# Gated linear attention with an ELU layer in float32: the output layer's matmuls regrouped, and a new written order for the first units

## The chip, the core and the metric

The kernel runs on one core of a Trainium2 chip. Its engines are TensorE (PE: matmul, with its weight loads listed apart as PEld), VectorE (DVE), ScalarE (ACT), GpSimd (POOL) and SyncE (SP), which here only issues DMAs. Each engine works through its own queue in order and waits on semaphores. The metric is the device time of one execution in microseconds (us); the figure to be forecast is the median over the runs.

## The reference

Shapes are B=4 sequences, H=8 heads, S=768 steps, D=48 channels; all in float32, with the two weight matrices given in float64.

```python
mag = np.sqrt(a_re * a_re + a_im * a_im)
scale = np.minimum(mag, 0.999) / (mag + 1e-06)
a_re_n, a_im_n = a_re * scale, a_im * scale
for t in range(S):                                   # complex decay per channel d
    new_re = ar * S_re - ai * S_im
    new_im = ar * S_im + ai * S_re
    S_re, S_im = new_re + k[t] (outer) v[t], new_im
    y[:, :, t] = q[t] @ S_re
x = y.transpose(0, 2, 1, 3).reshape(3072, 384)
h = x @ w_in                                         # 384 -> 2048
g = np.where(h > 0.0, h, np.exp(np.minimum(h, 0.0)) - 1.0)
out = g @ w_out                                      # 2048 -> 384
```

## The kernel before, in words

**Units.** The work is cut into 12 units (`NU`). A unit is 128 steps of two of the four sequences, so 256 tokens; `where(u)` says which. Units u and u+2 hold the same two sequences, one block of steps further on, so a unit needs the angles carried from unit u-2 (`carry`, a one-row DMA) and the states (`state`).

**One unit.** `squares` to `slopes`, `angles` and `carried` turn a_re, a_im into logarithms of magnitudes and angles. `decays` sums the logarithms over the steps with a triangular matmul (L873 for u>1, in `quartered`) and takes their exponentials E and F on ScalarE (L883). `turns` sums the angles the same way (L832) and DVE takes away whole turns; the result is `z`. `waves` makes sines and cosines on ScalarE (L949 to L953), `scaled` multiplies k by F and q by E, `gated` multiplies both by sine and cosine (kg, qg). `transposed` turns kg and qg over through TensorE (L984), with copies by ScalarE (L985). `scores` (L992), `states` (L1016, with updates on DVE at L1027 and POOL at L1029) and `values` (L1039, L1046) make the attention output for each sequence n; `seam` moves the last channels into place by DMA. `noted` records the least a_re and the largest |a_im| with two DVE reductions (unit 1: on ScalarE).

**The two layers.** `inner(u, f)` computes 256 hidden channels for the unit's 256 tokens: 6 matmuls of 256 columns (L1091) into one of three PSUM buffers named mlp. `elu(u, f)` takes two ScalarE steps and one on DVE (L1100 to L1102) into the tile g, of which a unit has two halves (`x["g", 0]`, `x["g", 1]`), from four buffers (tags g0 and g1, two each). `project(u, n, f0, f1)` is the output layer for the 128 tokens of sequence n: for each of 16 blocks f, one matmul with 128 weights columns of g and 384 columns of w_out (L1112), summed in one mlp buffer; then one ScalarE copy (L1118) and one store (L1120).

**Weights.** `fetch` loads float64 weights; `rounded` (called by `convert`, one DVE operation at a time, five for each of 16 chunks, L39 to L49 and L651) rounds them to float32. Later `test_fetch` loads all the weights a second time and `test` reduces them on DVE (L677): 16 pieces of 768 elements a partition, with two buffers. `verdict` combines what was noted; in the rare case that some value lies outside what the fast path takes, a general path behind an `If` runs instead. It doesn't run here.

**The order.** Nothing schedules the instructions but a list. `first` is written out by hand for units 0 to 2 and part of 3. All that follows comes from `plan`: every step has a place in slots (16 to a unit), and steps are issued in the order of their places: `decays_of`, `gates_of`, `values_of`, `layer_of`. Each engine's queue has its instructions in this order. `warm(n)` are matmuls without a use, to keep TensorE busy in the start.

Of the kernel before, what the change touches and what calls it, by code (L numbers as in the profile page):

```python
# [31 lines left out]
WF = 2  # L32

# [471 lines left out]
def kernel(  # L505
# [55 lines left out]
    NR = 2 * NI * NF // (NI * WF)  # L561
    seen = cst.tile([C, 2 * NU + NR], FP32, name="seen")
    least, smallest, most = seen[:, 0:NU], seen[:, NU : NU + NR], seen[:, NU + NR :]
    off = cst.tile([C, 2], FP32, name="off")
# [92 lines left out]
    def test_fetch(m):  # L657

        t = sb.tile([C, WF * DM, 2], U32, tag="w64", bufs=2, name="w64")
        if m < NR // 2:  # L660
            n = WF * DM // NI
            nc.sync.dma_start(
                out=t.rearrange("p (i n) two -> p i (n two)", i=NI),
                in_=moe_w_in[:, ds(2 * m * n, 2 * n)].rearrange("(i p) n -> p i n", p=C),
            )
        else:
            nc.sync.dma_start(
                out=t.rearrange("p (f n) two -> p f (n two)", f=WF),
                in_=moe_w_out[ts(m - NR // 2, WF * C)].rearrange("(f p) n -> p f n", p=C),
            )  # L670
        tested.append((m, t))
# [21 lines left out]
    def begun(u):  # L693
        keys = ("w", "m2", "sq", "t", "th", "z"), ("m2", "e", "sq", "w", "t", "th")
        for key in keys[u] if u < 2 else ("m2", "sq"):
            nat[u][key] = new("n", 6)

# [5 lines left out]
    def joined(u):  # L703

        x = nat[u]
        if u > 0:
            products(u).tensor_tensor(out=x["m2"], in0=x["m2"], in1=x["sq"], op=ALU.add)  # L707
            return
        x["both"] = [work([C, HD]) for n in range(NB)]
        for key in ("m2", "sq"):  # L710
            for n in range(NB):
                nc.tensor.matmul(
                    x["both"][n], lhsT=ident, rhs=flat(x[key][:, n : n + 1]),
                    start=(key == "m2"), stop=(key == "sq"),
                )

    def logarithms(u):
# [4 lines left out]
        if u == 0:  # L722
            for n in range(NB):
                nc.scalar.activation(
                    out=flat(lm[:, n : n + 1]), in_=x["both"][n], func=AF.Ln
                )
            return
# [5 lines left out]
    def powers(u):  # L733
        x = nat[u]
        if u == 0:
            x["e"] = x["m2"]
            for n in range(NB):
                nc.scalar.activation(
                    out=x["e"][:, n], in_=x["m2"][:, n], func=AF.Exp, scale=-0.5, bias=ln_eps
                )  # L740
# [8 lines left out]
    def ratios(u):  # L749
        x = nat[u]  # L750
        if u == 0:
            for n in range(NB):
                t = x["t"][:, n]
                nc.vector.tensor_tensor(out=t, in0=x["ai"][:, n], in1=t, op=ALU.mult)
            return
        w, t = x["w"], x["t"]
# [3 lines left out]
    def lengths(u):  # L760

        x = nat[u]
        if u == 0:
            nc.vector.tensor_scalar(
                out=x["w"], in0=x["m2"], scalar1=2 * float(np.log(CAP)), scalar2=None,
                op0=ALU.min,
# [15 lines left out]
    def noted(u, part=None):  # L782
# [3 lines left out]
        if u == 1:  # L786
            sq = nat[u]["sq"]
            for n, (x, scale, bias) in enumerate(((sq, 1.0, most_sq), (ar, -1.0, least_re))):
                nc.scalar.activation(
                    out=sq, in_=x, func=AF.Relu, scale=scale, bias=bias,  # L790
                    accum_out=off[:, n : n + 1],
                )
            return
        if part in (None, 0):
            nc.vector.tensor_reduce(
                out=least[:, u : u + 1], in_=flat(ar), axis=mybir.AxisListType.X, op=ALU.min
            )
        if part in (None, 1):
            nc.vector.tensor_reduce(
                out=most[:, u : u + 1], in_=flat(ai), axis=mybir.AxisListType.X, op=ALU.max,  # L800
                apply_absolute_value=True,
            )
# [3 lines left out]
    def angles(u):  # L806
        x = nat[u]
        if u == 0:
            for n in range(NB):
                nc.scalar.activation(out=x["th"][:, n], in_=x["t"][:, n], func=AF.Arctan)  # L810
# [15 lines left out]
    def turns(u):  # L826
        x = nat[u]
        if u > 0:
            x["z"] = new("n", 6)
        for n in range(NB):  # L830
            t = work([C, HD])
            nc.tensor.matmul(  # L832
                t, lhsT=sum_turns, rhs=x["th"][:, n].rearrange("p h d -> p (h d)"),
                start=True, stop=True,
            )
            r = new("rnd", 1, [C, HD])
            nc.vector.tensor_scalar(
                out=r, in0=t, scalar1=MAGIC, scalar2=MAGIC, op0=ALU.add, op1=ALU.subtract
            )
            nc.vector.tensor_tensor(  # L840
                out=x["z"][:, n].rearrange("p h d -> p (h d)"), in0=t, in1=r, op=ALU.subtract
            )
            if u < 2:
                if n == 0:
                    x["cs"] = new("cs", 1, [C, NB * H, 2, D])
                nc.vector.tensor_scalar(
                    out=x["cs"][:, n * H : (n + 1) * H, 0].bitcast(U32),
                    in0=x["z"][:, n].bitcast(U32), scalar1=0x7FFFFFFF, scalar2=None,
                    op0=ALU.bitwise_and,
                )  # L850
        nxt = u + B // NB
        if nxt < NU:
            carry[nxt] = new("carry", 2, [1, NB * HD])
            nc.gpsimd.dma_start(out=carry[nxt], in_=flat(x["z"])[C - 1 : C])  # L854

    def sums():
        x = nat[0]
        x["sums"] = [
            work([C, HD], "mlp") for n in range(NB)
        ]  # L860
        for n in range(NB):
            nc.tensor.matmul(
                x["sums"][n], lhsT=sum_logs, rhs=flat(x["w"][:, n : n + 1]),
                start=True, stop=False,
            )
# [26 lines left out]

    def decays(u):
# [443 lines left out]
```

## Time and profile before

| | |
|---|---|
| median of 9 runs | 726.92 us (723.76 to 732.7) |
| the profiled execution | 724.98 us, span 723.3 us |
| PE busy | 693.9 us (96%), 6240 records |
| PE weight loads busy | 512.0 us (71%) |
| DVE busy | 311.2 us (43%) |
| ACT busy | 398.5 us (55%) |
| POOL busy | 197.5 us (27%) |
| output layer (L1112) on PE | 768 records, 260.7 us busy |
| hidden layer (L1091) on PE | 1152 records, 262.6 us busy |

A float32 matmul stands in the trace as two records. A record's mean duration (491 ns for the output layer) holds its time in the pipeline; what it costs in a row of its like is the distance from one to the next, which the chain of work that ended last gives: a group's time by its count. "PE mlp L1112 x8" in the chain is eight records, four matmuls. In the groups of instructions, the columns are line, engine, operation, output<-inputs, shapes, count, then busy us and mean ns, and the idle time just before with what ended it. In the instructions in order of time: start us, us, engine, line, operation, output<-inputs, count, and in brackets the idle time before and what ended it.

### The profile page before, as it was taken

The numbers are of one execution on the slowest core, as the hardware profiler recorded it, in microseconds if no ns is written. First come the engines' busy times: TensorE is split into PE (matmuls) and PEld (weight loads), VectorE is DVE, ScalarE is ACT, GpSimd is POOL, SyncE is SP. The second block draws the span as 40 slices with busy tenths as digits, with TensorE's granted clock in tenths as the row PEclk, the third lists the DMA queues.
The fourth block names the chain that finished last, engine by engine and source line by source line (L and its number), as shares of the span: only waits on it lengthen the run. The fifth ranks groups of instructions, "written<-read, shape, count | busy, mean of one in ns | idle before, by whom it ended". The sixth has DMA issues, their size and how long they took to land.

```text
span 723.3 us, 14664 instructions
## 1 busy us (share of the span) xinstructions
PE 693.9 (96%) x6240; PEld 512.0 (71%) x6240; DVE 311.2 (43%) x426; ACT 398.5 (55%) x617; POOL 197.5 (27%) x207
## 2 busy tenths in 40 slices
PE   6889999977999999999999999999999999999996
PEld 4667785556866876876875875875885886786773
DVE  6889899554415324324324324423423323420120
ACT  6675361597466465565664674665666556550220
POOL 2000000056234134224324414414416306302000
PEclk9999999999999999999999999999999999999999
DMA  9964964430902902902902902812832722000000
GB/s 163 169 113 90 190 187 131 93 62 9 146 11 73 152 2 64 162 2 61 159 8 61 136 32 62 115 52 61 93 73 61 109 58 62 12 1 18 11 1 27
DMA packets 143110, 55.92 MB, mean 77 GB/s; under 512 B 128532, under 2 KB 132796, under 8 KB 143036
## 3 DMA queue, kind: packets, MB, share of 16 engines
q1 hardware_dynamic: 139456, 53.52, 39.2%
q0 software_dynamic: 3360, 1.22, 1.5%
q8 instruction: 51, 0.84, 0.5%
q14 instruction: 23, 0.19, 0.1%
q10 hardware_dynamic: 220, 0.14, 0.1%
HBM read 48.88 MB, written 4.78 MB: 74 GB/s over the span
## 4 chain that ended last, share of the span: by engine, by line
PE 84%; DVE 4%; SPq 3%; DMA 3%; issue 2%; POOL 2%; ACT 1%; ACTq 0%; POOLq 0%; DVEq 0%
PE mlp L1112 35%; PE mlp L1091 33%; PE w L984 5%; PE w L992 3%; PE w L1016 3%; PE y L1046 3%; SPq L594 2%; PE y L1039 2%; PE w L832 2%; DMA x<-y 1%; PE w L873 1%; DMA w<-in_moe_w_in_dram 1%; DMA w<-in_a_im_dram 1%; SPq L640 0%; POOL n L707 0%
## 5 line engine op out<-in xcount | busy, mean ns | idle before, releaser
L1091 PE MATMUL mlp<-x,w_in 128*128 128x256 f32 x1152 | 262.6, 383 | 3.2 <-DMA x<-y 1.9
L1112 PE MATMUL mlp<-w_out,g 128*128 128x384 f32 x768 | 260.7, 491 | 0.0
L1091 PEld LDWEIGHTS mlp<-x,w_in 128*128 128x128 f32 x1152 | 215.7, 191 | 35.4 <-issue 3.3
L1112 PEld LDWEIGHTS mlp<-w_out,g 128*128 128x128 f32 x768 | 142.1, 190 | 96.3 <-issue 4.8
L1102 DVE SCALAR_TENSOR_TENSOR g<-ee,mlp 128x512 f32<-128x512 f32 x96 | 65.9, 687 | 175.9 <-ACT ee L1101 162.9
L1100 ACT ACTIVATE ee<-mlp 128x512 f32<-128x512 f32 x96 | 57.4, 597 | 127.8 <-PE mlp L1091 123.3
L1029 POOL TENSOR_TENSOR S<-S,T 128x384 f32<-128x384 f32 x36 | 35.7, 992 | 183.3 <-DVE S L1027 183.3
L1101 ACT ACTIVATE ee<-ee 128x512 f32<-128x512 f32 x96 | 60.5, 630 | 2.9
L854 POOL DMA_DIRECT2D carry<-n x10 | 5.1, 506 | 159.2 <-DVE n L840 159.2
L1071 POOL DMA_DIRECT2D x<-y x65 | 31.9, 497 | 37.9 <-ACT y L1058 37.9
L1054 ACT COPY x<-y 128x384 f32<-128x384 f32 x24 | 11.5, 479 | 52.9 <-PE y L1046 52.9
L1027 DVE TENSOR_TENSOR S<-w,S 128x384 f32<-128x384 f32 x38 | 21.1, 556 | 44.7 <-PE w L1016 29.2
L1118 ACT COPY o<-mlp 128x384 f32<-128x384 f32 x24 | 11.3, 473 | 52.5 <-PE mlp L1112 48.4
L969 POOL TENSOR_TENSOR kg<-k,cs 128x1536 f32<-128x1536 f32 x9 | 35.7, 3969 | 14.2 <-issue 14.1
L997 DVE TENSOR_TENSOR a<-w,mask 128x512 f32<-128x512 f32 x24 | 16.5, 687 | 44.1 <-PE w L992 44.1
L707 POOL TENSOR_TENSOR n<-n 128x768 f32<-128x768 f32 x9 | 17.5, 1944 | 63.5 <-ACT n L701 63.5
L949 ACT ACTIVATE cs<-n 128x768 f32<-128x768 f32 (+1 forms) x14 | 10.5, 752 | 41.7 <-DVE n L840 41.7
L992 PEld LDWEIGHTS w<-qt,kt 128*64 128x64 f32 x768 | 24.4, 137 | 11.6 <-ACT n L701 4.4
L992 PE MATMUL w<-qt,kt 128*64 128x64 f32 x768 | 27.7, 225 | 2.6 <-ACT qt L985 1.5
L883 ACT ACTIVATE n<-w 64x384 f32<-64x384 f32 (+1 forms) x60 | 28.1, 486 | 3.5 <-PE w L873 2.7
L1016 PEld LDWEIGHTS w<-vn,kg 64*64 64x64 f32 x1280 | 22.7, 134 | 8.4 <-issue 8.1
L984 PE MATMUL w<-ident,kg 128*128 128x128 f32 x192 | 25.9, 277 | 1.8 <-DVE kg L969 1.7
(139 smaller groups left out, 781.0 us busy)
## 6 DMA issues: line engine op xcount, KB each, us to landing
w<-in_moe_w_out_dram SPq DMA_DIRECT2D x16, 768.0 KB
w<-in_moe_w_in_dram SPq DMA_DIRECT2D x8, 768.0 KB
w<-in_moe_w_in_dram SPq DMA_DIRECT2D x16, 288.0 KB
vn<-in_v_dram SPq DMA_DIRECT2D x24, 192.0 KB
out_dram<-o SPq DMA_DIRECT2D x24, 192.0 KB
ar<-in_a_re_dram SPq DMA_DIRECT2D x22, 192.0 KB
ai<-in_a_im_dram SPq DMA_DIRECT2D x22, 192.0 KB
q<-in_q_dram SPq DMA_DIRECT2D x22, 192.0 KB
```

Of the source, the lines that this page charges most:

```text
L883: nc.scalar.activation(out=flat(x[key][to, n : n + 1]), in_=t[of], func=AF.Exp, scale=sign)
L969: eng.tensor_tensor(out=to[:, :, :, 0:D], in0=each.unsqueeze(2).to_broadcast([C, step * H, 2, D]), in1=x["cs"][:, n * H : (n + step) * H], ...
L984: nc.tensor.transpose(t[:, h], of, ident)
L992: nc.tensor.matmul(t[ts(c, L), h], lhsT=x["kt", n][:, h, ts(c, L)], rhs=x["qt", n][:, h, ts(c, L)], start=True, stop=True,)
L1016: nc.tensor.matmul(g[ts(i, HP), h], lhsT=gates["k"][ts(c, L), n, h, i], rhs=vn[u % 2][ts(c, L), n, ts(h, D)], start=True, stop=True,)
L1029: eng.tensor_tensor(out=new_s, in0=new_s, in1=wide, op=ALU.mult)
L1071: eng.dma_start(out=x["x"][ds(j * HP + D, G), i], in_=x["y"][ds(j * HP + i * G, G)])
L1091: nc.tensor.matmul(t[:, e], lhsT=w_in[:, i, ts(f + e, C)], rhs=x["x"][:, i], start=(i == 0), stop=(i == NI - 1),)
L1100: nc.scalar.activation(out=e, in_=t, func=AF.Relu, scale=-1.0)
L1101: nc.scalar.activation(out=e, in_=e, func=AF.Exp, scale=-1.0)
L1102: nc.vector.scalar_tensor_tensor(out=x["g", f // 8][:, f % 8 : f % 8 + 2], in0=e, scalar=-1.0, in1=t, op0=ALU.add, op1=ALU.max)
L1112: nc.tensor.matmul(x["o", n], lhsT=x["g", f // 8][:, f % 8, ts(n, C)], rhs=w_out[:, f], start=(f == 0), stop=(f == NF - 1),)
```

## The change

**Seven half products.** From unit 2 on, the output layer is one step of Strassen's scheme. The hidden tile is cut in two by sequence (i) and by even and odd blocks f (j), into X(i, j); w_out by even and odd blocks (j) and by halves of its 384 columns, into Y(j, n). The eight block products X(i, j) Y(j, n) become seven, each of 192 columns over 8 blocks for 128 tokens. `opened` and `combined` make the weights' differences once; `folded` makes the sums of hidden tiles for each unit and half h; `product` runs one product for one half and adds results on DVE. Products share the three mlp buffers (`bank`), two of 192 columns to a buffer. Results leave in four stores a unit of 192 columns. Since two g1 buffers become `spare`, units from 2 on use the two g0 buffers alone.

**First unit by tiles.** Unit 0's steps up to `waves` and `scaled` take a sequence n (or a key) at a time, and the list places them singly. `noted` runs on ScalarE for units 0, 1 and 2.

**Two units' output layers together.** In the list, the pieces of `project` of units 0 and 1 stand between each other and between the steps of units 2 and 3.

**Tests.** `test_fetch` and `test` take half as much at a time (`WT = 1`), 32 times, into one buffer in `spare[1]`.

```diff
-        if u == 1:
+        if u < OFF:
...
...
-            x["g", f // 8] = sb.tile([C, 8, GT], FP32, tag="g" + str(u % 2), bufs=2, name="g")
+            x["g", f // 8] = sb.tile([C, 8, GT], FP32, tag="g" + str(u % 2 * (u < 2)), bufs=2, name="g")
...
         if f1 == NF:
-            o = new("o", 1, [C, DM])
-            nc.scalar.copy(out=o, in_=x["o", n])
-            nc.sync.dma_start(out=out[ds((b + n) * S + s, C)], in_=o)
+            for m in range(2):
+                o = new("o", 2, [C, HN])
+                nc.scalar.copy(out=o, in_=x["o", n][:, ts(m, HN)])
+                nc.sync.dma_start(out=out[ds((b + n) * S + s, C), ts(m, HN)], in_=o)
...
+    def Y(j, n):
+        return w_out.rearrange("p (m j) n -> p m j n", j=2)[:, :, j, ts(n, HN)]
...
+    def opened():
+        for n in range(2):
+            spare.append(sb.tile([C, 8 * GT], FP32, tag="g1", bufs=2, name="g"))
...
+    def T_of(k, h):
+        if k == 4:
+            return spare[4 + h]
+        return (spare[2] if k == 1 else spare[3] if k == 2 else Y(0, 1))[:, ts(h, P // 2)]
...
+    def combined(k, h):
+        of = {
+            1: (Y(0, 1), Y(0, 0)), 2: (Y(1, 1), spare[2]), 4: (spare[3], Y(1, 0)),
+            3: (Y(1, 1), Y(0, 1)),
+        }[k]
+        a, b = (x[:, ts(h, P // 2)] for x in of)
+        nc.vector.tensor_tensor(out=T_of(k, h), in0=a, in1=b, op=ALU.subtract)
...
+    def X(u, h, i, j):
+        return nat[u]["g", h].rearrange("p (m j) (i t) -> p m j i t", j=2, i=2)[:, :, j, i]
...
+    def S_of(u, k, h):
+        if k == 1:
+            return X(u, h, 1, 0)
+        n, at = {2: (0, 0), 3: (0, 1), 4: (1, 0)}[k]
...
+    def folded(u, h):
+        for k, a, b, op in (
+            (3, X(u, h, 0, 0), X(u, h, 1, 0), ALU.subtract),
+            (1, X(u, h, 1, 0), X(u, h, 1, 1), ALU.add),
+            (2, S_of(u, 1, h), X(u, h, 0, 0), ALU.subtract),
+            (4, X(u, h, 0, 1), S_of(u, 2, h), ALU.subtract),
+        ):
+            nc.vector.tensor_tensor(out=S_of(u, k, h), in0=a, in1=b, op=op)
+
+    def product(u, k, h):
+        bank, n, first = {
+            1: (0, 0, True), 2: (0, 0, False), 6: (0, 1, False), 5: (1, 0, True),
+            7: (1, 1, False), 3: (1, 0, False), 4: (2, 0, True),
+        }[k]
+        if first and h == 0:
+            x["p", bank] = work([C, 2, HN], "mlp")
+        to = x["p", bank][:, n]
+        a = {
+            1: lambda: X(u, h, 0, 0), 2: lambda: X(u, h, 0, 1), 3: lambda: S_of(u, 4, h),
+            4: lambda: X(u, h, 1, 1), 5: lambda: S_of(u, 1, h), 6: lambda: S_of(u, 2, h),
+            7: lambda: S_of(u, 3, h),
+        }[k]()
+        if k < 4:
+            b = Y(*((0, 0), (1, 0), (1, 1))[k - 1])[:, ts(h, P // 2)]
+        else:
+            b = T_of({4: 4, 5: 1, 6: 2, 7: 3}[k], h)
+        for m in range(P // 2):
+            nc.tensor.matmul(
+                to, lhsT=a[:, m], rhs=b[:, m], start=(first and h == 0 and m == 0), stop=False,
+                skip_group_check=True,
+            )
+        if h == 0 or k in (4, 5):
+            return
+        if k == 1:
+            x["u"] = new("ee", 2, [C, 2, GT])
+            nc.scalar.copy(out=x["u"][:, 0, 0:HN], in_=to)
+            return
+        u2, u3 = (x["u"][:, n, 0:HN] for n in range(2))
+        if k == 6:
+            nc.vector.tensor_tensor(out=u2, in0=to, in1=u2, op=ALU.add)
+            return
...
+        if k == 7:
+            nc.vector.tensor_tensor(out=u3, in0=to, in1=u2, op=ALU.add)
+            done(1, 1, u3, x["p", 1][:, 0], ALU.add)
+            done(1, 0, u3, x["p", 2][:, 0], ALU.subtract)
+        elif k == 2:
+            done(0, 0, to, None)
+        else:
+            done(0, 1, to, u2, ALU.add)
...
-        (project, 1, 1, 4, 8), (carried, 2), (lengths, 2), (load_v, 3), (decays, 2), (turns, 2),
-        (scaled, 2), (waves, 2), (gated, 2), (project, 1, 1, 8, 12), (project, 1, 1, 12, 16),
...
+        (project, 0, 1, 4, 8), (convert,), (project, 0, 0, 8, 12), (decays, 2),
+        (project, 1, 0, 4, 8), (turns, 2), (waves, 2), (ends, 2), *4 * [(convert,)], (scaled, 2),
...
+        (inner, 2, 2), (waves, 3), (gated, 3), (opened,), (combined, 1, 0), (combined, 2, 0),
+        (combined, 4, 0), (combined, 3, 0), (combined, 1, 1), (combined, 2, 1), (combined, 4, 1),
+        (combined, 3, 1), (load_v, 3), (elu, 2, 0), (elu, 2, 2), (ends, 3), (inner, 2, 4),
...
-        for m in range(NF // 2):
-            n, q4 = divmod(m, NF // 4)
-            put(at_p[m], project, u, n, 4 * q4, 4 * q4 + 4)
+        put(at_h[3], folded, u, 0)
+        put(at_h[7], folded, u, 1)
+        ks = [(1, 0), (4, 0), (1, 1), (4, 1)] + [(k, h) for k in (6, 5, 7, 2, 3) for h in range(2)]
+        for m, (k, h) in enumerate(ks):
+            put(at_p[0] + m * len(at_p) / len(ks), product, u, k, h)
...
-            decays_of(u, r + 11, r + 12, r + 12, r + 13.4, r + 13.5, r + 14.5, r + 14.6, r + 15.5, r + 15.5)
+            decays_of(u, r + 11, r + 12, r + 12, r + 13.4, r + 13.5, r + 14.9, r + 16.7, r + 15.5, r + 16.6)
...
-        put(40 + 8 * m, test_fetch, m)
-        put(47 + 8 * m, test)
+        put(40 + 4 * m, test_fetch, m)
+        put(43 + 4 * m, test)
```

## The prediction

> **What bounds the kernel now.** I read the page's first parts, then the chain that ended last in order of time, then instructions in order of time. The page:
>
> ```profile
> PE 693.9 (96%) x6240; PEld 512.0 (71%) x6240; DVE 311.2 (43%) x426; ACT 398.5 (55%) x617; POOL 197.5 (27%) x207
> PE 84%; DVE 4%; SPq 3%; DMA 3%; issue 2%; POOL 2%; ACT 1%; ACTq 0%; POOLq 0%; DVEq 0%
> L1112 PE MATMUL mlp<-w_out,g 128*128 128x384 f32 x768 | 260.7, 491 | 0.0
> L1112 PEld LDWEIGHTS mlp<-w_out,g 128*128 128x128 f32 x768 | 142.1, 190 | 96.3 <-issue 4.8
> ```
>
> TensorE carries 84% of the chain, and the output layer (L1112) never waited. A float32 matmul is two records: 12 units x 32 output matmuls give the 768. The chain repeats from unit to unit:
>
> ```profile
> 397.97 7.77 PE mlp L1091 x36
> ...
> 442.09 7.94 PE mlp L1112 x24
> 450.03 1.29 PE w L832 x4
> 451.32 2.58 PE mlp L1112 x8
> 453.90 7.77 PE mlp L1091 x36
> ```
>
> From 397.97 to 453.90 is 55.93 us for one unit, with almost no idle. 2.58/8 gives 323 ns per output record; 7.77/36 gives 216 ns for 256 columns. Ahead of this the chain has a start: unit 2's first hidden matmuls come at 172.62. Busy time by windows of 20 us (TensorE, its loads, DVE, ACT, POOL):
>
> ```profile
> 80.00:100.00 20.00, 19.50 (x91) 17.21 (x92) 18.03 (x25) 8.80 (x15) 0.00 (x0) 1.00 0.82 197
> 100.00:120.00 20.00, 20.00 (x71) 13.13 (x70) 19.38 (x27) 7.28 (x10) 0.00 (x0) 1.00 0.52 165
> 160.00:180.00 20.00, 15.64 (x234) 12.09 (x229) 9.08 (x13) 16.09 (x26) 13.80 (x13) 0.91 0.03 8
> ```
>
> DVE is nearly full (12.9, 17.6, 18.1, 17.5 in the four windows before): it rounds weights until 127.5 and paces the first two units. From about 142 to 172 TensorE waits again and again for unit 2's and unit 3's decays. From unit 2's hidden layer on it is the bound itself.
>
> What stands closest behind TensorE in the cycle, in order of time:
>
> ```profile
> 385.29 0.88 PE L873 MATMUL w<-n,sum_logs 64*64 64x384 f32 x8
> 386.21 2.38 ACT L883 ACTIVATE n<-w 128x384 f32<-128x384 f32 x5 [0.34 <-PE w L873]
> 389.11 1.28 ACT L814 ACT_TABLE_LOAD   x1
> 390.40 0.84 ACT L814 ACTIVATE n<-n 128x768 f32<-128x768 f32 x1
> 391.28 0.95 DVE L820 SCALAR_TENSOR_TENSOR n<-carry,n 1x768 f32<-1x768 f32 x1 [2.25 <-ACT n L814]
> 393.62 1.16 PEld L832 LDWEIGHTS w<-n,sum_turns 128*128 128x128 f32 x4
> ```
>
> The angles of the unit after next are ready 392.23-385.29 = 6.9 us after L873 starts; TensorE comes for them after 8.3. Margin 1.4 us.
>
> **What the skill says.** The Trainium skill, "TensorE: Matmul & The Clock Gate", section "LDWEIGHTS (loading the stationary operand)", prices a load at columns/1.2, an estimated 107 ns for 128; "Back-to-back issue gap" there says the spacing is set by load and matmul together. The trace agrees roughly: records of 128 columns with a full load each follow at 2.93/24 = 122 ns and 1.02/8 = 128 ns,
>
> ```profile
> 21.70 2.93 PE L1190 MATMUL mlp<-ident 128*128 128x128 f32 x24
> 257.75 1.02 PE w L984 x8
> ```
>
> so the 190 ns of the PEld row is not a spacing. "VectorE: DVE Perf Modes", "Why `tensor_tensor` can't do 2×_2P or 4×": float32 with two tensors gets one element a cycle; the trace agrees (768 elements: 0.95 us with two tensors, 0.56 with one). "ScalarE: Activation LUTs", "What ACT_TABLE_LOAD costs": 1283 ns; the trace shows 1.28.
>
> **The change, part by part.**
>
> (1) *Seven half products*, units 2 to 11. Gone: 32 matmuls x 2 records x 323 ns = 20.67 us a unit. Added: 7 products x 2 halves x 4 matmuls = 56, of 192 columns: 112 records. No row has 192 columns. From 256 and 384 (216, 323) the line gives 163; half way between 128 and 256 (125, 216) gives 170. I take 163, since at 192 the stream should hide a load of under 128. 112 x 0.163 = 18.2 us: 2.5 us less a unit, 25 over ten (at 170: 16).
>
> (2) *Sums for them.* Eight folds a unit on DVE, 512 elements: 0.69 each by L997 (same size, two inputs), 5.5 us; five sums of 192 elements at about 0.36 (half the 384's 0.56 and some fixed part), 1.8. DVE goes from some 19.6 to 27 us of a 53 us cycle. The first four folds (2.8 us) stand between two ELU steps: the next ELU was at 358.07 and comes near 358.6, while the hidden buffer that it frees is wanted at 361.6. The other four are done before TensorE reaches the product that reads them, because P1 and P4 (5.2 us with scores and states between) need none. Cost zero while those covers hold, else up to 2.8 each. The first product P3 adds into a bank column that DVE must have read as P5; P2 (two halves, 2.6 us) stands between, against about 1.1 of DVE: zero too. ScalarE's copies stay about 1 us a unit. g's four buffers become two; the next unit's first ELU follows the last product on TensorE anyway: zero.
>
> (3) *Waits in the cycle.* Between L873 and L832 TensorE now has 40 records of 163 = 6.5 us in place of 24 x 323: with L873's 0.9 it arrives 7.4 us after L873 starts, the angles after 6.9. Margin 0.5 of 1.4. Behind a late L832 stand P2, P3 and the next unit's hidden matmuls. Ahead of L837 on DVE now stand both `noted` reductions (1.9) and three sums (1.1): z slips by about 2 us. On ScalarE the P1+P2 copy stands ahead of the sines and wants an `o` buffer whose store only left at 6.9+1.9+1.1 = 9.9 us; store 0.36, landing 3.2 (as x<-y's median), copy 0.3, table 1.28, three waves 2.6, gating on DVE 1.76: 19.4. TensorE wants gated q at 7.4+1.3+3.9+7.8 = 20.4. Between transposed k and scores the cover falls from 2.58 to 1.30 us, the copies need about 1.1. Everything just fits; I put 0.3 us a unit on it over nine units, 2.7. Bounds: none, and 2 a unit.
>
> (4) *Weight differences*, once: eight DVE operations of 768 elements, 7.6 us, queued behind unit 3's gated q and ahead of unit 2's first ELU. From unit 3's L832: sines end near +6.8, gating +8.6, differences +16.2, ELU +16.9. TensorE has three hidden groups (7.8) and q and k transposes (2.1), and then wants the first buffer, at about +12: a stall near 4.8. The present first cycle (172.6 to 230.2) holds 1.7 of stall already, part of it replaced: I take +1.5 net of that unit's own 2.5.
>
> (5) *The start.* Decays by tile take ScalarE's two needless table loads out and bring gated k of unit 0 from 27.1 to about 25.3; but DVE has rounded less by then (1.5 us of work against 4.0), and it paces. DVE's 110.8 us busy up to 127.5: less 1.9 (unit 0's `noted` now on ScalarE, where it stands ahead of the copies of transposed k), plus 0.5 for splits, less 10.5 of rounding now after unit 1's last ELU, is 98.9; with 16.6 of idle (as now) or 13 it is 112 to 115. The last hidden matmuls end some 2 us before, 110. Then 24 output matmuls (15.5), L873 and four more: unit 2's L832 at 129 (now 142.8). From there TensorE has 34 us of work (32 output matmuls 20.7, attention 13.3) plus stalls: gated k comes 9.3 us after L832 against 6.5 (2.8), k copies 1; and at the end unit 3's angles stand on ScalarE behind the last output copies, 4.2 us after the last output matmul, where 0.9 is covered (3.3). With L832 itself 43: unit 2's hidden matmuls at 172, now 172.6. The two units' outputs fill what is now idle in 142 to 172, but the decays of units 2 and 3 are no shorter. -0.6; bounds -13 (all of DVE's waits and these stalls gone) and +5.
>
> (6) *Tests by half tiles*: 32 of 384 elements for 16 of 768, one buffer: SP waits for each test before the next fetch, behind which stores and loads queue. A fetch has three slots (10 us) to land; SP's ten loads take 12.3 (344.7 to 357) of 53. Zero, or 1 us a unit if late.
>
> Sum: -0.6 + 1.5 - 9 x 2.47 + 2.7 = -18.6. The profiled execution took 724.98 (span 723.3), the median of nine is 726.92; I take 18.6 off both: span 704.7, median **708.3**.
>
> **Rivals.**
> - *The cycle's waits decide* (0.2): any margin of (3) overdrawn by 1 to 2 us a unit, 9 to 18 in all. For it: three margins under 1 us. Against: it needs the store to land over 4 us. 714 to 723, say 717.
> - *The start gains* (0.14): DVE's idle shrinks and unit 2's hidden matmuls come at 160: 696. For: 16.6 us idle there. Against: stalls of (5).
> - *Loads set the pace* (0.05), the one that ends slower: each record costs its load, not its columns, at the PEld row's 190 ns. 112 x 0.190 = 21.3, 0.6 more a unit than now; with -0.6, +4, +2.7: 739. From 180 ns on (206.7-6.1 over 1120 records) the change loses. The 122 ns of L1190 speaks against it.
> - That the products aren't fewer columns can't be: 56 x 192 = 10,752 for 12,288.
>
> My own case has 0.61, 702 to 713. Leaving out the tails, 8 in 10 lies in **698 to 719**. 0.5% (3.6 us) is about what a measurement can tell. Faster 0.92, within 0.03 (the far end of the waits), slower 0.05.
>
> **What would show it.** Product records spaced 163 ns apart and cycles near 53.7 us: (1). TensorE's idle ahead of L832, of gated q's transposes and of scores, under 0.5 us a unit: (3). One stall of about 5 us after unit 2's third hidden group, released by DVE: (4). Unit 2's hidden matmuls at 172: (5). Wrong if spacing is 175 or more, cycles are over 55, or that start is before 164.

## The result, and the profile after

The changed kernel takes **718.41 us** (median of 10 runs, 714.23 to 721.05), the kernel before 727.60 us beside it (31 runs): a ratio of 0.9866, 95% interval 0.9837 to 0.9894. It is faster by 1.3%, some 9 us, half of the 18.6 forecast. The profiled execution took 716.9 us, span 715.2, against 724.98 and 723.3: 8.1 us less.

The first lines are from the page of the kernel after: busy time, the chain by engine, and the output layer's largest group (L1216, which was L1112).

```profile
PE 676.8 (95%) x6720; PEld 581.3 (81%) x6720; DVE 393.6 (55%) x579; ACT 400.2 (56%) x631; POOL 197.6 (28%) x207
PE 74%; DVE 4%; ACT 2%; issue 1%; POOL 0%; ACTq 0%; DVEq 0%
L1216 PE MATMUL mlp<-w_out,g 128*128 128x192 f32 x640 | 111.3, 328 | 0.0
L1235 ACT COPY o<-mlp 128x192 f32<-128x192 f32 x10 | 3.2, 318 | 63.9 <-DMA out_dram<-o 42.7
```

TensorE is still busy 95% of the time. The last line looks alarming: ScalarE idles 6.4 us a unit ahead of this copy, 4.3 of them until a store has left the `o` buffer. It costs nothing, as the cycle shows. In the chain of the kernel after, in order of time (start us, us, what):

```profile
297.63 7.77 PE mlp L1110 x36
306.28 2.59 PE mlp L1110 x12
...
339.23 6.70 PE mlp L1216 x40
345.93 1.29 PE w L832 x4
347.22 3.90 PE mlp L1216 x24
351.12 7.77 PE mlp L1110 x36
```

A unit begins at 297.63 and the next at 351.12: 53.49 us, where it was 55.93. The product records follow at 3.90/24 = 163 ns; the group of 40 holds a pause of 0.2 us beside that. The instructions of one such cycle in order of time, around L832:

```profile
343.46 0.84 ACT L815 ACTIVATE n<-n 128x768 f32<-128x768 f32 x1
344.33 0.95 DVE L821 SCALAR_TENSOR_TENSOR n<-carry,n 1x768 f32<-1x768 f32 x1 [4.12 <-ACT n L815]
345.76 1.45 PE L832 MATMUL w<-n,sum_turns 128*128 128x384 f32 x4
353.64 1.76 DVE L988 TENSOR_TENSOR qg<-q,cs 128x1536 f32<-128x1536 f32 x1 [1.80 <-ACT cs L966]
358.72 1.04 PE L1003 MATMUL w<-ident,qg 128*128 128x128 f32 x8
```

The angles are ready at 345.28, TensorE takes them at 345.76: a margin of 0.48 us. Gated q is ready at 355.40 and wanted at 358.72. TensorE waits for nobody in this cycle, nor in the six others like it.

Unit 2 differs. From its first hidden matmul to unit 3's there were 57.57 us before (172.62 to 230.19) and are 70.15 now (174.00 to 244.15). Both ends in the chains, of the kernel before

```profile
172.62 9.41 PE mlp L1091 x36
...
230.19 7.77 PE mlp L1091 x36
```

and, for unit 3, of the kernel after:

```profile
244.15 7.77 PE mlp L1110 x36
```

The kernel after, instructions in order of time, cut to what lies on the path:

```profile
174.00 8.90 PE L1110 MATMUL mlp<-x,w_in 128*128 128x256 f32 x36
178.40 1.76 DVE L988 TENSOR_TENSOR qg<-q,cs 128x1536 f32<-128x1536 f32 x1 [2.14 <-ACT cs L966]
178.50 4.99 POOL L988 TENSOR_TENSOR kg<-k,cs 128x1536 f32<-128x1536 f32 x1 [0.49 <-POOL k L976]
180.08 4.23 DVE L1174 TENSOR_TENSOR w<-w_out 128x768 f32<-128x768 f32 x1
184.34 0.96 DVE L1174 TENSOR_TENSOR w<-w_out,w 128x768 f32<-128x768 f32 x1
...
191.54 5.25 PE L1110 MATMUL mlp<-x,w_in 128*128 128x256 f32 x12 [6.87 <-DVE g L1121]
...
218.15 10.08 DVE L1194 TENSOR_TENSOR g<-g 128x512 f32<-128x512 f32 x8
...
229.71 0.88 PE L883 MATMUL w<-n,sum_logs 64*64 64x384 f32 x8 [2.07 <-DVE n L772]
230.51 4.54 PE L1216 MATMUL mlp<-w,g 128*128 128x192 f32 x16
```

Four things are to be seen. The first weight difference takes 4.23 us where its like takes 0.95. TensorE waits 6.87 us behind the eight of them. The 12 hidden records after this wait take 5.25 us, where 12 take 2.59 in the cycle. And the eight folds of unit 2 come in one run of 10.08 us after its last ELU step, with waits of 1.25, 0.32, 0.67 and 2.07 us on TensorE around it and slow products behind it (16 records in 4.54 us, elsewhere 2.87).

The spans, taken apart at the first hidden matmuls of units 2 and 3 and of unit 10 (us):

| stretch | before | after | change | forecast |
|---|---|---|---|---|
| start, up to unit 2's hidden matmuls | 172.62 | 174.00 | +1.4 | -0.6 |
| unit 2's cycle | 57.57 | 70.15 | +12.6 | +1.5 |
| seven cycles, units 3 to 9 | 391.46 | 374.37 | -17.1 | } -19.5 |
| unit 10 to the end | 101.65 | 96.68 | -5.0 | } |

The forecast's 19.5 is nine units at 2.47 less its 2.7 for waits. So the loss against the forecast sits in unit 2's cycle (11.1 us) and in the start (2.0); the later units gave 2.5 more than forecast.

### The profile page after: what moved, and what is told of

It reads as the page before. It is cut to its first block, busy times and chain, and to the rows that moved or that the text cites. A ratio compares the mean times of both kernels' runs of the same rounds, so it can differ in the third digit from the quotient of the medians.

```text
span 715.2 us, 15901 instructions
## 1 busy us (share of the span) xinstructions
PE 676.8 (95%) x6720; PEld 581.3 (81%) x6720; DVE 393.6 (55%) x579; ACT 400.2 (56%) x631; POOL 197.6 (28%) x207
## 3 DMA queue, kind: packets, MB, share of 16 engines
q0 software_dynamic: 3360, 1.22, 1.3%
## 4 chain that ended last, share of the span: by engine, by line
PE 74%; DVE 4%; ACT 2%; issue 1%; POOL 0%; ACTq 0%; DVEq 0%
PE mlp L1110 29%; PE mlp L1216 26%; PE w L1003 5%; PE w L1011 3%; PE w L1035 3%; PE y L1065 3%; PE y L1058 2%; PE w L832 2%; PE mlp L1131 2%; DVE g L1194 1%; DVE w L1174 1%; PE w L883 1%; PE w L1131 0%; ACT n L893 0%; ACT cs L966 0%
## 5 line engine op out<-in xcount | busy, mean ns | idle before, releaser
L1216 PE MATMUL mlp<-w_out,g 128*128 128x192 f32 x640 | 111.3, 328 | 0.0
L1216 PEld LDWEIGHTS mlp<-w_out,g 128*128 128x128 f32 x640 | 104.3, 190 | 2.7
L1048 POOL TENSOR_TENSOR S<-S,T 128x384 f32<-128x384 f32 x36 | 29.8, 829 | 180.4 <-DVE S L1046 180.4
L1194 DVE TENSOR_TENSOR g<-g 128x512 f32<-128x512 f32 x80 | 59.7, 748 | 2.7
L1216 PE MATMUL mlp<-w,g 128*128 128x192 f32 x320 | 58.7, 338 | 1.0 <-DVE g L1194 0.7
L1216 PEld LDWEIGHTS mlp<-w,g 128*128 128x128 f32 x320 | 53.2, 195 | 6.8 <-issue 4.8
L988 POOL TENSOR_TENSOR kg<-k,cs 128x1536 f32<-128x1536 f32 x9 | 39.2, 4354 | 15.8 <-issue 15.2
L1131 PE MATMUL mlp<-w_out,g 128*128 128x384 f32 x96 | 33.1, 493 | 2.0 <-DVE g L1121 2.0
L716 POOL TENSOR_TENSOR n<-n 128x768 f32<-128x768 f32 x9 | 16.3, 1814 | 61.4 <-ACT n L710 61.4
L1216 PE MATMUL mlp<-wt,g 128*128 128x192 f32 x160 | 30.2, 332 | 1.2 <-DVE g L1121 1.2
L1004 ACT COPY kt<-w 128x512 f32<-128x512 f32 x48 | 25.7, 586 | 7.8 <-PE w L1003 6.4
```

Of the source, the lines that this page charges most:

```text
L988: eng.tensor_tensor(out=to[:, :, :, 0:D], in0=each.unsqueeze(2).to_broadcast([C, step * H, 2, D]), in1=x["cs"][:, n * H : (n + step) * H], ...
L1048: eng.tensor_tensor(out=new_s, in0=new_s, in1=wide, op=ALU.mult)
L1131: nc.tensor.matmul(x["o", n], lhsT=x["g", f // 8][:, f % 8, ts(n, C)], rhs=w_out[:, f], start=(f == 0), stop=(f == NF - 1),)
L1194: nc.vector.tensor_tensor(out=S_of(u, k, h), in0=a, in1=b, op=op)
L1216: nc.tensor.matmul(to, lhsT=a[:, m], rhs=b[:, m], start=(first and h == 0 and m == 0), stop=False, skip_group_check=True,)
```

## The experiments

My theory: the seven products save their 2.47 us in every unit, and unit 2 loses some 15 us to its own order of work: the differences queued ahead of its first ELU step, the first of them blocked by GpSimd, the folds in one run, and TensorE's granted clock after the waits (1.00 is full speed; it is 0.50 in places). Rivals: the fuller load costs the time and it only moves from wait to wait; the new start order itself costs it; the folds bound the cycle.

In every table the "cycle" is that of unit 2. The seven cycles behind it took 53.46 to 53.49 us each in every kernel with seven products but the one with doubled folds.

### Spreading the differences, and moving four folds

```diff
-        (inner, 2, 2), (waves, 3), (gated, 3), (opened,), (combined, 1, 0), (combined, 2, 0),
-        (combined, 4, 0), (combined, 3, 0), (combined, 1, 1), (combined, 2, 1), (combined, 4, 1),
-        (combined, 3, 1), (load_v, 3), (elu, 2, 0), (elu, 2, 2), (ends, 3), (inner, 2, 4),
+        (inner, 2, 2), (waves, 3), (gated, 3), (opened,), (load_v, 3), (elu, 2, 0), (elu, 2, 2),
+        (combined, 1, 0), (ends, 3), (inner, 2, 4),
...
```

The others stand behind later ELU steps: (2,0) behind (elu,2,4), (4,0) behind (elu,2,6), (3,0) and (1,1) behind (elu,2,8), (2,1) behind (elu,2,10), (4,1) and (3,1) behind (elu,2,12).

> Only the places of the eight weight differences change: one or two after each of unit 2's ELU steps in place of all eight ahead of the first. My theory (the missing time sits in unit 2's cycle: the wait of 6.87 us behind the differences, and 12 records at half speed after it, 5.25 us for 2.59): both go, some 9.5 us, less 1 or 2 for a difference that now holds an ELU back; span near 707, ratio to the kernel before 0.974 to 0.978, and the first hidden groups of unit 2 run at 216 ns a record. Rival 1 (what the change costs is its fuller load, and a wait taken away only comes back at the next one): 713 or more. Rival 2 (the eight folds in one run are the costly part): 715, unchanged.

The folds alone:

```diff
-        (inner, 2, 12), (elu, 2, 10), (transposed, 3, "k", 1), (transposed, 3, "q", 1),
+        (inner, 2, 12), (elu, 2, 10), (folded, 2, 0), (transposed, 3, "k", 1), (transposed, 3, "q", 1),
```

> Only unit 2's first four folds move: from behind its last ELU step to behind its sixth, where VectorE stands idle for 7.6 us. My theory: the waits behind the run of folds (1.25, 0.32, 0.67 and 2.07 us) lose about 2 us and the products after them the 1.7 us that they took too long: 712 to 713, ratio 0.982 to 0.985. Rival 1: the time comes back in the next wait, 715. Rival 2 (the folds are the costly part): 708 or less.

Both:

> Both moves together, nothing else. My theory: unit 2's cycle comes from 70.4 us near the 57.6 of the kernel before less 2.5: span 703 to 707, ratio 0.970 to 0.977. Rival 1 (the time only moves on to other waits): 712 or more. Rival 2: as the early folds alone.

| | median us | ratio to before, 95% | span | unit 2 starts | cycle |
|---|---|---|---|---|---|
| changed kernel | 718.41 | 0.9866 (0.9837 to 0.9894) | 715.2 | 174.00 | 70.15 |
| differences spread | 709.30 | 0.9769 (0.9716 to 0.9822) | 708.5 | 175.01 | 62.20 |
| four folds earlier | 713.00 | 0.9842 (0.9794 to 0.9890) | 710.1 | 172.75 | 65.76 |
| both | 705.55 | 0.9719 (0.9663 to 0.9775) | 703.5 | 174.79 | 57.40 |

The cycle falls by 7.95, 4.39 and, with both, 12.75 us: the two about add up, and the largest waits left in the cycle with both are 1.24 and 1.68 us. That is what my theory had said, and against the rival of the moving wait. A cycle is that of one execution, and its length scatters with the clock: the kernel tried last, which only adds matmuls to unit 0, has the changed kernel's unit 2 and took 67.41 us for it. The medians, over several runs, fell by 9.1, 5.4 and 12.9 us and say the same. The instructions that do the sums are the same; only their places differ.

### The new start with the old output layer

The changed kernel, with `project` for every unit, no differences and no folds, g in its four buffers, and the tests loading into a tile of their own:

```diff
-            x["g", f // 8] = sb.tile([C, 8, GT], FP32, tag="g" + str(u % 2 * (u < 2)), bufs=2, name="g")
+            x["g", f // 8] = sb.tile([C, 8, GT], FP32, tag="g" + str(u % 2), bufs=2, name="g")
...
+        for m in range(NF // 2):
+            n, q4 = divmod(m, NF // 4)
+            put(at_p[m], project, u, n, 4 * q4, 4 * q4 + 4)
```

> The changed kernel with the output layer of before for every unit: no weight differences, no folds, four g buffers; the new start and the tests by half tiles stay. My theory (the start is worth nothing, and unit 2's cycle suffers only from what the seven products need): unit 2's hidden matmuls at 173 to 174, its cycle 57 to 58 us, span 723 to 726, ratio 0.998 to 1.004. Rival 1 (the new start itself costs unit 2's cycle some 10 us): 731 or more, ratio 1.01. Rival 2 (the start gains and the gain is lost later to the seven products): 718 or less.

725.11 us, ratio 0.9979 (0.9958 to 1.0001); span 720.9; unit 2 starts at 171.32, its cycle takes 56.25, the later ones 55.93. So the new start doesn't cost unit 2's cycle anything (it is 1.3 us shorter than before), and is worth some 1.5 us itself (0 to 3 by the interval). The rival of the start order falls.

### What made the first difference slow

```diff
-            eng = products(u) if key == "k" else nc.vector
+            eng = products(u) if key == "k" and u != 3 else nc.vector
```

> The changed kernel, with unit 3's gated k alone computed on VectorE (1.76 us) and not on GpSimd (4.99 us). My theory (the first weight difference took 4.23 us for 0.95 because it and GpSimd's gating exclude each other): that difference takes 0.95 us, so the eight end 3.28 - 1.76 = 1.5 us sooner, the wait behind them falls from 6.87 to about 5.3, span 713.5 to 714.5. Rival (the first difference waits for its buffer or its weights): it stays over 4 us, the differences end 1.8 us later, span about 717.

The kernel with unit 3's kg on VectorE, instructions in order of time:

```profile
179.95 1.76 DVE L988 TENSOR_TENSOR kg<-k,cs 128x1536 f32<-128x1536 f32 x1 [2.21 <-POOL k L976]
183.29 0.95 DVE L1174 TENSOR_TENSOR w<-w_out 128x768 f32<-128x768 f32 x1
191.47 5.49 PE L1110 MATMUL mlp<-x,w_in 128*128 128x256 f32 x12 [5.52 <-DVE g L1121]
```

The first difference takes 0.95 us once GpSimd doesn't work beside it, and the wait falls from 6.87 to 5.52 (5.3 expected). The cycle fell by 1.05, 1.5 expected; the span (715.7) did not, because this execution's start was 1.5 us later. The median, 717.83, and its ratio of 0.9860 (0.9805 to 0.9915) don't tell it from the changed kernel, so the durations carry this reading.

The Trainium skill, "SBUF — State Buffer", section "SBUF: two separate sides", says why: VectorE operations with two SBUF inputs and GpSimd operations that read SBUF share a pair of ports under an exclusive lock, held for a whole instruction. The trace agrees, to within 0.15 us. VectorE's qg runs from 178.40 to 180.16; kg, shown from 178.50, ends at 183.49, which is 3.33 us after qg (the median of kg in the kernel before is 3.47). The difference, shown from 180.08, ends 0.82 us after kg. So the 4.99 and the 4.23 us are each a wait for the other engine and one run of about ordinary length. The kernel before had shown the half of it, in the same place of unit 3:

```profile
177.33 1.76 DVE L969 TENSOR_TENSOR qg<-q,cs 128x1536 f32<-128x1536 f32 x1 [2.61 <-ACT cs L953]
177.44 4.97 POOL L969 TENSOR_TENSOR kg<-k,cs 128x1536 f32<-128x1536 f32 x1 [1.89 <-issue]
```

The run of folds in the changed kernel met the same. Three of its eight folds each stand beside an operation of GpSimd and take 2.1 to 2.2 us; the other five take the ordinary 0.69:

```profile
217.91 1.81 POOL L716 TENSOR_TENSOR n<-n 128x768 f32<-128x768 f32 x1
218.15 2.12 DVE L1194 TENSOR_TENSOR g<-g 128x512 f32<-128x512 f32 x1
223.65 1.82 POOL L759 TENSOR_TENSOR n<-ar,n 128x768 f32<-128x768 f32 x1 [3.94 <-ACT n L747]
223.81 2.21 DVE L1194 TENSOR_TENSOR g<-g 128x512 f32<-128x512 f32 x1
225.55 2.13 POOL L760 TENSOR_TENSOR n<-ai,n 128x768 f32<-128x768 f32 x1
226.05 2.18 DVE L1194 TENSOR_TENSOR g<-g 128x512 f32<-128x512 f32 x1
```

That is 4.4 of the run's 10.08 us. With four folds earlier one fold is hit (2.00 us), with both moves none, so the moves took away this loss too; no run separates it from that of the place.

### What made the records after the wait slow

```diff
+    def kept_warm(n):
+        t = work([C, C])
+        for _ in range(n):
+            nc.tensor.matmul(t, lhsT=ident, rhs=ident, start=True, stop=True)
...
-        (transposed, 3, "q", 0), (elu, 2, 4), (transposed, 3, "k", 0), (inner, 2, 6), (elu, 2, 6),
+        (transposed, 3, "q", 0), (elu, 2, 4), (transposed, 3, "k", 0), (kept_warm, 28), (inner, 2, 6), (elu, 2, 6),
```

> The changed kernel, with 28 matmuls of the identity (nobody reads them) on TensorE in the wait ahead of unit 2's fourth hidden group; the wait itself, for VectorE, stays. My theory (the 12 records behind it took 5.25 us and not 2.6 because the clock falls in an idle of 6.9 us): they take 2.6 to 2.8, some 2.5 us less, span 712 to 713.5. Rival 1 (they are slow because they still wait piece by piece for buffers): 5.2 us as before, 715. Rival 2 (the clock comes back only with full load, and the filling is too thin): between the two.

The kernel with the wait filled, instructions in order of time:

```profile
191.97 2.86 PE L1110 MATMUL mlp<-x,w_in 128*128 128x256 f32 x12 [0.64 <-DVE g L1121]
...
227.75 0.88 PE L883 MATMUL w<-n,sum_logs 64*64 64x384 f32 x8 [2.06 <-DVE n L772]
228.56 2.87 PE L1216 MATMUL mlp<-w,g 128*128 128x192 f32 x16
```

713.86 us, ratio 0.9799 (0.9742 to 0.9857), span 711.9, cycle 65.94. TensorE reaches these records no sooner, but they take 2.86 us for 5.25: 2.4 us, by work that nobody reads. There was a second gain that I hadn't expected: behind the wait of 2.06 us ahead of L883 the 16 product records took 2.87 us and not 4.54, though that wait is as long as before. It need not be the filling's doing: the kernel tried last, which fills nothing in unit 2, has 2.87 us behind the same wait too. The Trainium skill, "TensorE: Matmul & The Clock Gate", section "What's actually happening", has an idle TensorE fall to half its clock after an idle window of about 3.4 us, in windows that run on their own. The first point agrees: 5.25 us is 437 ns a record, twice the 216 of the cycle. The traces show the windows as well: the granted clock changes only in steps of 3.41 us. In the changed kernel it is 0.50 from 189.59 to 196.42 (two steps), behind a step without any work on TensorE, and from 230.55 to 233.96 (one), behind a step that holds the whole wait of 2.07 us and 1.34 us of work. In the kernel with the wait filled a step ends inside that wait, at 226.24, and the clock stays at 1.00. But in the kernel tried last the step from 227.93 to 231.34 holds all but the last 0.1 us of this wait, and the clock stays at 1.00 all the same. So a wait shorter than a step can halve the clock, and how much idle time in a step it takes stays open.

### How much cover the folds have

```diff
-            (3, X(u, h, 0, 0), X(u, h, 1, 0), ALU.subtract),
+            *5 * [(3, X(u, h, 0, 0), X(u, h, 1, 0), ALU.subtract)],
```

> The changed kernel with the first of the four folds of each half computed five times, so twelve folds more than... eight more operations of 0.69 us a unit, 5.5 us: VectorE's folds doubled, sums unchanged. My theory (in the steady cycles the folds are hidden): cycles of units 3 to 9 stay within 0.5 us of 53.5 as long as the four extra ones at a half are covered; only unit 2's cycle and the last unit grow, by 3 to 6 us each. Rival (the folds bound the cycle or sit on its edge): cycles of 56 us or more, span 735 or more.

(Four more operations a half, eight a unit. A fold is covered while TensorE has other work to do.) One execution: 732.61 us, span 730.8. Cycles 54.31 us (the last two 54.68 and 54.94) for 53.49: 0.8 us a unit, where at most 0.5 was expected. VectorE had 7.1 us more a unit and not 5.5, since one fold in each cycle now stands beside GpSimd's L716 and takes 2.31 us. A run of eight folds ahead of the masked scores holds them, these hold the states on GpSimd, and TensorE then waits, 0.43 us of the 0.8 in this place:

```profile
332.42 7.39 DVE L1194 TENSOR_TENSOR g<-g 128x512 f32<-128x512 f32 x8
342.31 0.99 PE L1065 MATMUL y<-qt,S 128*48 128x64 f32 x28 [0.43 <-POOL S L1048]
```

The folds are hidden as they are, but the cover has less left than the 4.5 us by which this run grew (7.39 us for 2.87). Unit 2's cycle grew by 4.1 us, and the end, from unit 10 on, by 2.8, about as expected from folds in a place without cover.

### Looking for the rest of unit 2's cycle

With both moves the cycle was still 57.40; 57.57 less the 2.47 of the products would be 55.1. The last two differences stood beside operations of GpSimd there and took 1.22 and 2.57 us, ahead of unit 2's last ELU step. The first five differences stay as spread above; then

```diff
-        (inner, 2, 12), (elu, 2, 10), (transposed, 3, "k", 1), (transposed, 3, "q", 1),
-        (inner, 2, 14), (values, 3, 0), (scores, 3, 1), (states, 3, 1), (elu, 2, 12),
-        (elu, 2, 14),
+        (inner, 2, 12), (elu, 2, 10), (folded, 2, 0), (combined, 2, 1), (transposed, 3, "k", 1),
+        (transposed, 3, "q", 1), (inner, 2, 14), (combined, 4, 1), (elu, 2, 12), (combined, 3, 1),
+        (values, 3, 0), (elu, 2, 14), (scores, 3, 1), (states, 3, 1),
```

> As both moves together, but the last differences and the first four folds go into VectorE's wait behind unit 2's sixth ELU step, and its last two ELU steps ahead of unit 3's second masked scores. My theory (what is left of unit 2's cycle, 57.4 us against 53.5 later, are the waits of 1.24 and 1.68 us for late ELU steps): these two go, span 700 to 702, unit 2's cycle 54.5 to 55.5 us. Rival (the second scores and states of unit 3 are held back by the earlier ELU steps instead): 703.5 or more, no gain on both moves.

705.61 us, ratio 0.9692 (0.9638 to 0.9746), span 703.7, cycle 60.38. The two waits went, and the cycle became 3 us longer than with both moves: here the time did move on, though not to where the rival had it. This kernel, in order of time:

```profile
209.66 0.84 ACT L736 ACTIVATE n<-n 128x768 f32<-128x768 f32 x1 [3.21 <-POOL n L716]
212.65 0.83 ACT L747 ACTIVATE n<-n 128x768 f32<-128x768 f32 x1
213.38 0.30 ACT L1224 COPY ee<-mlp 128x192 f32<-128x192 f32 x1
213.73 5.49 PE L1216 MATMUL mlp<-w,g 128*128 128x192 f32 x16 [3.70 <-ACT ee L1224]
```

ScalarE waits for GpSimd's sum for unit 4 (L716), takes the logarithms and exponentials, and only then copies product 1; product 6, in the same bank, waits for that copy, and again the 16 records after a wait of 3.70 us run at half speed. Two ways out:

```diff
-        ks = [(1, 0), (4, 0), (1, 1), (4, 1)] + [(k, h) for k in (6, 5, 7, 2, 3) for h in range(2)]
+        ks = [(1, 0), (4, 0), (1, 1), (4, 1)] + [(k, h) for k in (5, 6, 7, 2, 3) for h in range(2)]
```

> As the spread with more, but in every unit product 5 (which has a bank of its own) goes ahead of product 6 (which shares product 1's bank and waits for ScalarE's copy of product 1). My theory (the 3.70 us that product 6 of unit 2 waited, and the 16 records after it at 5.49 us for 2.6, come from that copy standing behind unit 4's logarithms on ScalarE): product 5 covers 2.6 us of the wait, the clock stays, unit 2's cycle falls from 60.4 to about 56, the later cycles stay at 53.5; span less the start's own time down by 4. Rival (product 5 then waits as long, for its folds or its bank): no gain, and 1 us or more lost in every cycle.

and, in the list,

```diff
-        (values, 3, 0), (elu, 2, 14), (scores, 3, 1), (states, 3, 1),
+        (values, 3, 0), (elu, 2, 14), (scores, 3, 1), (states, 3, 1),
+        (product, 2, 1, 0), (product, 2, 4, 0), (product, 2, 1, 1),
```

> As the spread with more, but unit 2's products 1 and 4 (first half) and 1 (second half) are issued ahead of unit 4's decays, so that ScalarE's copy of product 1 stands ahead of unit 4's logarithms. My theory: the wait of 3.70 us and the slow records after it go, about 6 us in all, unit 2's cycle near 55. Rival 1 (the logarithms, now behind the copy, come too late for the sums of unit 4's logarithms instead): a wait of 2 to 4 us moves to the sums, cycle 57 to 58. Rival 2 (product 4's second half or the folds hold as long): 60, unchanged.

| | median us | ratio to before, 95% | span | unit 2 starts | cycle |
|---|---|---|---|---|---|
| spread with more | 705.61 | 0.9692 (0.9638 to 0.9746) | 703.7 | 171.75 | 60.38 |
| product 5 ahead of 6 | 705.64 | 0.9711 (0.9655 to 0.9767) | 703.9 | 175.85 | 55.09 |
| copy ahead | 703.10 | 0.9663 (0.9609 to 0.9717) | 703.2 | 174.11 | 58.06 |

Product 5 ahead takes 5.3 us out of the cycle, and costs none of the later cycles; but the span did not show it, for two reasons: this start was 4.1 us later, and from unit 10 on 98.6 us were needed and not 97.2. The cause is in order of time, near the end of this kernel:

```profile
688.86 0.24 PE L1269 MATMUL w<-seen,ones 128*1 128x44 f32 x2 [1.25 <-DVE seen L1265]
```

The verdict on the tests stands on VectorE behind product 6's sum, which is now later. With the copy ahead, the first rival was right: the wait moved to the sums of unit 4's logarithms (2.51 us at L883), and the records after it were slow once more. So the order of 5 and 6 was changed in unit 2 alone:

```diff
+        ks = [(1, 0), (4, 0), (1, 1), (4, 1)] + [(k, h) for k in ((5, 6) if u == 2 else (6, 5)) + (7, 2, 3) for h in range(2)]
```

> The spread with more, with product 5 ahead of product 6 in unit 2 alone. My theory (with that order in every unit the last one lost 1.25 us, because product 6's sum on VectorE stands ahead of the verdict on the tests, and unit 2's cycle was 55.1): unit 2's cycle 55 to 55.5, no wait ahead of the verdict's matmul, so 527.5 to 528 us from unit 2's hidden matmuls to the end; with these at 171 to 176 a span of 699 to 703.5, ratio to the kernel before 0.963 to 0.969. Rival (the lost time at the end came from somewhere else): as with that order in every unit, 0.970 or more.

**701.49 us** (6 runs, 700.01 to 705.61), ratio **0.9672** (0.9632 to 0.9711), against 725.00 of the kernel before beside it. Span 699.7; unit 2 starts at 173.62, its cycle is 55.07, and from there to the end it takes 526.1 us (527.5 to 528 expected). No wait stands ahead of the verdict. Its unit 2, in order of time:

```profile
204.95 1.57 PE L1216 MATMUL mlp<-w_out,g 128*128 128x192 f32 x8
212.00 2.87 PE L1216 MATMUL mlp<-w,g 128*128 128x192 f32 x16
215.93 0.88 PE L883 MATMUL w<-n,sum_logs 64*64 64x384 f32 x8 [1.05 <-DVE n L772]
216.73 2.87 PE L1216 MATMUL mlp<-w,g 128*128 128x192 f32 x16
```

55.07 is 57.57 less 2.5, as much as every other unit gains; against the new start with the old output layer, whose unit 2 took 56.25, it is 1.2.

### The start's own scatter

In kernels whose instructions are the same up to unit 2, its hidden matmuls came at 171.3 to 175.9, and TensorE's clock from 20 to 60 us differed too:

| kernel | mean clock 20 to 40, 40 to 60 | unit 2 starts |
|---|---|---|
| new start, old output layer | 1.00, 1.00 | 171.32 |
| spread with more | 0.97, 0.95 | 171.75 |
| four folds earlier | 0.86, 1.00 | 172.75 |
| changed kernel | 0.86, 0.91 | 174.00 |
| differences spread | 0.76, 0.82 | 175.01 |
| kg on VectorE | 0.76, 0.82 | 175.48 |

The other six start at 173.62 to 175.88, with clocks of 0.76 to 0.88 and 0.80 to 0.88. The two latest, at 175.85 and 175.88, have 0.86, 0.80 and 0.84, 0.84, so the clock doesn't account for all of it.

I tried to hold the clock, in the ends of unit 0's decays:

```diff
                     )
+                if u == 0:
+                    warm(3 + 3 * n)
             once = new("once", 1, [D, NB, C // L, H])
```

> The changed kernel, with 3 and 6 matmuls of the identity (nobody reads them) between the narrow matmuls of unit 0's decay ends, where TensorE has 32 two-column records and a wait of 1.5 to 1.7 us. My theory (the start's own scatter, unit 2's hidden matmuls at 171.3 to 175.5 in runs of the same start, comes from the clock, which in the slow starts falls to 0.5 from about 22 to 27 and again from 38 to 48): the clock stays 0.95 or more from 20 to 60, unit 2's hidden matmuls at 171 to 172.5, span 712.5 to 714. Rival (the clock in the start is a matter of the execution, or of a wait elsewhere): 0.76 to 0.91 as in most runs, 174 to 175.5, span 715 to 717.

717.62 us, ratio 0.9876 (0.9819 to 0.9932), span 715.6, unit 2 starts at 176.80. The clock, now 1.00 from 18 to 34, fell all the same to 0.50 from 36.8 to 47.0. This began in the following wait, at which the profile shows nothing that TensorE waited for:

```profile
37.58 1.63 PE L1037 MATMUL mlp<-vn,kg 64*64 64x48 f32 x51 [3.29 <-issue]
```

The same wait is 1.19 us in the kernel that started at 171.32, 2.53 in the one at 175.48 and 3.14 in the changed kernel. So the rival was right that there is a wait elsewhere, and the added matmuls brought nothing. What TensorE waits for there stays open, and so does what sets the start's length.

## Why the prediction was half right

The range held the result, the likeliest value was 10 us too low, and the reason is one term.

**(1) Seven half products: right.** 163 ns a record, as interpolated; 163 and not 170. The cycle gave 2.44 us, 2.47 worked out (2.42 with 163 exactly).

**(2) Sums for them: right in size, and zero in every cycle but unit 2's.** Folds of 0.69 us and sums of 0.36 as priced, but for unit 2's run of folds, 4.4 us longer beside GpSimd. What I did not check is that unit 2 has another order: its first four folds did not stand between two ELU steps, because the written list issues all of unit 2's hidden layer before the plan issues its folds. The cover I had named was gone there, and I had said what that would cost ("up to 2.8 each"); the four early folds alone gave 4.39 us back.

**(3) Waits in the cycle: too high.** The margin at L832 came out at 0.48 us where I had worked out 0.5. Gated q had 3.3 us to spare, not 1.0: the copy that waited for the store ran at 349.43, 11.1 us after L883 started, not 13.5. I put 2.7 us on waits and there were none.

**(4) Weight differences: the step that failed.** The place, the releaser and the sequence were right: one wait after the third hidden group and the transposes, released by VectorE's ELU step. Foreseen was unit 2's cycle 4.0 us above its best (a net of 1.5, and the unit's own 2.5); it was 15.1 above the 55.07 of the kernel with 5 ahead of 6 in unit 2 alone. Its parts are 6.87 us of wait (4.8 foreseen; the differences took 10.7 us and not 7.6, since the first was locked out by kg, while the gating before them ended 1 us sooner than I had taken), 2.7 of slow records behind it, 4.3 of waits around the run of folds (1.25 of them for the last ELU steps, which stayed with the four folds moved) and 1.7 of slow products: 15.5 by these waits and durations, for the 15.1. The waits at the folds belong to step (2). I priced eight operations by the ordinary duration on an engine taken as alone, though the trace of before had kg at 4.97 us beside VectorE's qg in this place and at 3.47 in six of its nine units; and I priced a wait as its own length, without what TensorE's clock adds after it.

**(5) The start: near.** Unit 2's L832 came at 130.6 (129 forecast), the wait at the end was 2.89 (3.3), that for kg 0.45 (2.8 foreseen). Its hidden matmuls came at 174.0 (172), with the clock at 0.86 from 20 to 40 us and 0.91 from 40 to 60; in an execution of the same start at full clock they came at 171.3.

**(6) Tests: zero, as taken.**

**The rivals.** "The cycle's waits decide" has a number close to the result (717) and is wrong all the same: it needed 1 to 2 us lost in every unit, and none was. "Loads set the pace" fell with the 163 ns. "The start gains" fell with 174.

## What to carry to other kernels

Price a one-time set-up where it stands, not by its sum: ask which engine's queue it enters, who stands behind it, and what runs beside it at that moment (an operation with two inputs on VectorE beside one on GpSimd took up to 3.3 us longer here); spread over a unit, these eight operations cost almost nothing. A unit written out by hand has other covers than the planned ones after it, so check each hidden cost in it anew. A wait on TensorE can cost its length and then more for the slow records behind it, and an order that is better in one unit (product 5 ahead of 6) can cost time in another.

## What I had not expected of the hardware

- VectorE and GpSimd operations side by side took turns: VectorE's 0.95 us became 4.23 and 0.69 became 2.2, and GpSimd's 3.47 became 4.99. The profile shows it as duration, not as a wait.
- After 6.87 us without work TensorE ran 12 records at 437 ns each, not 216. After a wait of 2.07 us its records were slow in the changed kernel and not in two others, and the clock changed only in steps of 3.41 us.
- A wait of 1.2 to 3.3 us in the start that the profile puts down to nothing differs from one execution to the next. The clock differs with it, and the start's length, by 4 us, mostly goes with the clock; what makes the wait stays open.
